# Attention with 128 weight columns for the scores, loads moved in the loop, and a rearranged passage from attention to the first expert block

## The chip, the cores and the metric

The kernel runs on one core of a Trainium2 chip. The metric is device microseconds of one execution; the kernel before has a median of 965.54 us in 3 runs (964.71 to 966.51). TensorE is written PE in the profile (PEld is its weight loads), VectorE DVE, ScalarE ACT, GpSimd POOL, SyncE SP.

## The reference

Causal attention over 4 batches, 12 heads, 448 positions and 64 dimensions a head, then two mixture-of-experts layers in sequence, each with 1792 tokens of 768 numbers, 8 experts, one expert a token, and 1024 hidden numbers. Everything is float32.

```
scores = where(causal, scale * q @ k.T, -1e9)
x      = softmax(scores) @ v                      # 1792 x 768
idx, gate = argmax / softmax of x_normed @ emb_normed.T / tau
x      = gate * (relu(x @ w1[idx]) @ w2[idx])     # first layer
idx, gate = argmax / softmax of x @ w_gate + bias[modality]
out    = gate * (relu(x @ w1'[idx]) @ w2'[idx])   # second layer
```

The routing of the first layer needs whole tokens, that is all twelve heads of a batch.

## The kernel before, in words

Attention works on 24 pairs of heads (`NPR`; six pairs a batch), each in four chunks of 112 query rows (`CP`). float32 products are made of two float32r parts, hi and lo: `split_pair` (L365) scales q and splits k and q on GpSimd, `split_v` (L379) splits v into three bfloat16 parts there. One round g of the loop from L763 works on four pairs at once: scores of pair g (`qk`, row maxima on VectorE, exponentials on ScalarE), the probabilities of pair g-1 as two float16 halves (`halves_hi` on ScalarE, `halves_lo` L424 on VectorE with both inputs in SBUF, DMA transposes of them on SP, and `last_chunk`, which transposes the last chunk on TensorE), the products with v of pair g-2 (`values`, then `combine`, which divides by the sums and writes x), and routing of pair g-3 (`route_t`: x transposed and split into xTh and xTl; `route_l`: its product with the expert embedding). Rounds 24 to 26 have no scores and finish the last pairs.

In `qk`, a chunk's scores are three products of q's 112 columns as weights (hi*hi, hi*lo, lo*hi), for two heads on the two halves of the rows, and one product of a 112 x 112 identity with the mask. hi and lo come from the pool `raw` with three buffers each; `r`, where k and q land, has four (`ld_p`), and v six.

The order of work is written out by hand: each engine and each DMA queue runs its instructions in program order. The loads of pair g+4 and of v of pair g+3 stand near the end of round g (L834 to L837), on SP's queue behind the transposes of `halves_hi(g)`. A batch's routing (`route1`, L629) is a generator; `tick` (L648) takes one step of it after certain VectorE operations, six in the rounds behind the last scores. `yield ALIGN` holds it until the top of the next round, where its products are put on TensorE. Its first part (`route_root`) takes roots of the squared norms, its second the expert of each token, ranks among the tokens of an expert, the softmax, counts, and four scatters by GpSimd. Batch b's routing starts when x of all its chunks has been stored and squared (`store_x`, `route_ss`, L808 to L816); for the third batch (b = 2) chunks 0, 1 and 2, 3 go out at the first, second and third round of the next batch.

From round 18 on, w1 of the expert with most tokens so far is loaded in six parts (`w1r`). Its float32r high parts `w1h` and low parts `w1l` are tiles of the pool `wb`, which is opened in round 24 when the memory of attention's probabilities is given back. GpSimd copies `w1h` 0 and 1, ScalarE 2 to 5; VectorE subtracts `w1l` 0 and 1 at the end of round 24 and 2, 3 and 4, 5 at the top of rounds 25 and 26. `warm` (L747) puts products of a constant on TensorE whose result nobody reads: eight (`WT`) in each of rounds 24 to 26, and six more (`WV`) ahead of `values` in rounds 24 and 25. `up` (L924) is the first product of an expert block: per half, 18 products of 512 columns, in the order L930, L931, L932 for each of six parts; L932 needs the low part of x (`xl`, L915 in `prep`).

Of the kernel before, what the change touches and what calls it, by code (L numbers as in the profile page):

```python
# [9 lines left out]
F32 = mybir.dt.float32  # L10
F32R = mybir.dt.float32r
BF16 = mybir.dt.bfloat16
# [3 lines left out]
AF = mybir.ActivationFunctionType  # L16
ALU = mybir.AluOpType
AX = mybir.AxisListType
# [5 lines left out]
P = 128  # L24
B, H, S, HD = 4, 12, 448, 64
CP, NCH = 112, 4
NT, D, F, E = 1792, 768, 1024, 8
KD, KF = D // P, F // P
# [13 lines left out]
WT = 8  # L42
WV = 6
# [12 lines left out]
def attention_two_moe_kernel(  # L56
# [34 lines left out]
    pool.memset(mask, 0.0)  # L91
    pool.affine_select(out=mask[:, :CP], in_=mask[:, :CP], compare_op=ALU.is_ge, fill=NEG, base=0,
                       pattern=[[-1, CP]], channel_multiplier=1)
    identb = const.tile([CP, CP], BF16, name="identb")
    vec.tensor_copy(identb, ident[:CP, :CP])
    iota_i = const.tile([P, JB * E], I32, name="iota_i")
    iota8 = const.tile([P, E], F32, name="iota8")
    pool.iota(iota_i[:, :E], pattern=[[1, E]], base=0, channel_multiplier=0)
# [43 lines left out]
    def pcopy(dst, src):  # L142
        pool.tensor_scalar(out=dst, in0=src, scalar1=1.0, scalar2=1.0, op0=ALU.mult, op1=ALU.mult)
# [149 lines left out]
    xb_p = right(st_v, "xb_p", 2)  # L293
    at_p = right(st_x, "at_p", 1)
    ld_p = right(st_q, "ld_p", 4)
    raw = right(st_q, "raw", 3)
    ps_s = st_q.enter_context(tc.tile_pool(name="ps_s", bufs=4, space=PSUM, side="right", reuse_waits="tile"))

    def clear_meta():
# [51 lines left out]
    PB = H // 2  # L351
    raws, spl, vrs, vss = {}, {}, {}, {}

    def load_pair(g):
        b, i = divmod(g, PB)
        r = ld_p.tile([P, 2, S], F32, tag="r", name=f"r{g}")
        nc.sync.dma_start(r, kqP[b, :, i])
        raws[g] = r

    def load_v(g):  # L360
        b, i = divmod(g, PB)
        vrs[g] = av_p.tile([CP, 2, NCH, HD], F32, tag="vr", name=f"vr{g}", bufs=6)
        nc.sync.dma_start(vrs[g], vh[b, :, 2 * i : 2 * i + 2])

    def split_pair(g, fast=False):  # L365
        r = raws.pop(g)
        (vec if fast else pool).tensor_scalar(out=r[:, 1], in0=r[:, 1], scalar1=-0.125, scalar2=1.0,
                                              op0=ALU.mult, op1=ALU.mult)
        hi = raw.tile([P, 2, S], F32R, tag="hi", name=f"hi{g}")
        lo = raw.tile([P, 2, S], F32R, tag="lo", name=f"lo{g}")  # L370
        spl[g] = hi[:, 0], lo[:, 0], hi[:, 1], lo[:, 1]
        if fast:
            vec.tensor_copy(hi, r)
            vec.tensor_sub(lo, r, hi.bitcast(F32))
        else:
            pcopy(hi, r)
            psub(lo, r, hi.bitcast(F32))
# [13 lines left out]
    def qk(g, c):  # L391

        kh, kl, qh, ql = spl[g]
        n = CP * (c + 1)
        cs = slice(c * CP, (c + 1) * CP)
        for e in range(2):
            scs[2 * g + e, c] = ps_s.tile([CP, 512], F32, tag="sc", name=f"sc{2 * g + e}_{c}")
        for st, (a, b) in enumerate(((qh, kh), (qh, kl), (ql, kh))):
            for e in range(2):
                rs = slice(e * HD, (e + 1) * HD)  # L400
                pe.matmul(scs[2 * g + e, c][:, :n], lhsT=a[rs, cs], rhs=b[rs, :n], start=(st == 0), stop=False)
        for e in range(2):
            pe.matmul(scs[2 * g + e, c][:, cs], lhsT=identb, rhs=mask[:, :CP], start=False, stop=True)  # L403

    def rowmax(h, c):
        if c == 0:
            nms[h] = sm_p.tile([CP, NCH], F32, tag="nm", name=f"nm{h}")
        vec.tensor_reduce(out=nms[h][:, c : c + 1], in_=scs[h, c][:, : CP * (c + 1)], axis=AX.X, op=ALU.min)  # L408

    def expo(h, c):  # L410
        n = CP * (c + 1)
        dst = exs[h // 2 % NEX][:, h % 2, boff[c] : boff[c] + c + 1].rearrange("p j k -> p (j k)")
        act.activation(dst, scs.pop((h, c))[:, :n], AF.Exp, bias=nms[h][:, c : c + 1], scale=-1.0)  # L413

    def transposed(dst, src):
        nc.sync.dma_start_transpose(dst[:, : 2 * ND * CP].rearrange("p (n q) -> p n q", q=CP),
# [264 lines left out]
    def split_w(which, his=None, los=None):  # L681
        drain(split_steps(which, his, los))
# [64 lines left out]
    def warm(ps, tag, n):  # L747

        wt = ps.tile([P, 512], F32, tag=tag, name="warm")
        for _ in range(n):  # L750
            pe.matmul(wt, lhsT=ones[:CP], rhs=mask, start=True, stop=True)
# [10 lines left out]

    for g in range(NPR + 3):  # L763
        t, v, r = g - 1, g - 2, g - 3
        if r == 0:
            drain(routing)
            routing = None
            vec.tensor_scalar_mul(tau_h, tau_t, 0.5)
            for b in range(B):
                vec.tensor_copy(mts[b][:, :, 3], mod_i[:, b * NCH : (b + 1) * NCH, 0])  # L770
# [7 lines left out]
        if g < NPR:  # L778
            for c in range(2):
                both(rowmax, g, c)  # L780
            for c in range(2):
                both(expo, g, c, ticks=False)
        if g == NPR + 1:
            split_w(1, (), (2, 3))
        if g == NPR + 2:
            split_w(1, (), (4, 5))
        if 0 <= t < NPR:
            halves_lo(t)
        next(late[0], None)
        if NPR <= g:  # L790
            warm(ps_T, "T", WT)
        if 0 <= r < NPR:
            if r == NPR - 1:
                for c in range(NCH):
                    route_ss(B - 1, c, xbs[B - 1], 2)
                last_root = route_root(B - 1)
                next(last_root)
            route_t(r, xbs[r // PB])
            if r == NPR - 2:
                for c in range(NCH):  # L800
                    route_ss(B - 1, c, xbs[B - 1], 1)
        next(late[0], None)
        if 0 <= v < NPR:
            if g > NPR - 1:
                warm(ps_T, "T", WV)
            values(v, 0)
        next(late[0], None)
        if PB <= r < NPR and r % PB < NCH:  # L808
            b = r // PB - 1
            c = -1  # L810
            for c in ((0,), (1,), (2,), (3,))[r % PB] if b < B - 2 else ((0,), (1,), (2, 3), ())[r % PB]:
                store_x(b, c)
                route_ss(b, c, xbs[b])
            if c == NCH - 1:
                drain(routing or ())
                routing = route1(b)  # L816
# [14 lines left out]
            combine(v, xbs[v // PB])  # L831
        if g < NPR:
            halves_hi(g)
        if g + 4 < NPR:  # L834
            load_pair(g + 4)
        if g + 3 < NPR:
            load_v(g + 3)  # L837
        if g + 2 < NPR:
            split_pair(g + 2)
        if g + 1 < NPR:  # L840
# [4 lines left out]
        if g == NPR - 1:  # L845
            st_q.close()
            ps_h = left("ps_h", 2, space=PSUM)
            ps_T = left("ps_T", 2, space=PSUM)
        if g == NPR:
            st_x.close()  # L850
            wb = left("wb", 1)
            w1h = [wb.tile([P, F], F32R, name=f"w1h{c}") for c in range(KD)]
            w1l = [wb.tile([P, F], F32R, name=f"w1l{c}") for c in range(KD)]
            w2r = [wb.tile([P, D], F32, name=f"w2r{f}") for f in range(KF)]
            m1.gather_early((0,), 2 * S)
            load_lead(m1, 2)
        if g == NPR:
            for k in range(2):
                pcopy(w1h[k], w1r[k])
            split_w(1, (2, 3, 4, 5), (0, 1))  # L860
    drain(routing)
    b = B - 1
    for c in range(NCH):
# [575 lines left out]
```

## Time and profile before

| | |
|---|---|
| median of 3 runs | 965.54 us (964.71 to 966.51) |
| profiled execution | 968.53 us, span 966.8 us |
| mean granted TensorE clock | 0.967 |
| busy: PE, PEld, DVE | 881.5, 761.0, 698.4 us |
| busy: ACT, POOL | 430.2, 472.4 us |
| scores of pair 0 start, of pair 23 end | 7.90, 242.8 us |
| first `up` starts | 275.23 us |

The profiled execution's span is from its first to its last instruction; the rest of its time lies around it. In a timeline a row gives the start in us from the span's start, the time it lasts, the engine, the line, the operation with output and inputs, and how many instructions were merged (x4); in brackets the idle time of the engine just before it and what ended it. In a busy table by stretch, the columns are the length, the busy time and count of PE, PEld, DVE, ACT and POOL, the granted clock, the DMA engines' share and GB/s.

### The profile page before, as it was taken

What the parts mean: (1) busy time and instruction counts of PE and PEld (TensorE: products, weight loads), DVE (VectorE), ACT (ScalarE), POOL (GpSimd) and SP (SyncE); (2) the same over time, 40 slices, a digit from 0 to 9 for tenths busy, and PEclk for the clock granted to TensorE, in tenths of its full rate; (3) what the DMA queues carried; (4) which work ended last, traced back from release to release, by engine and by line L of the source; (5) the groups of instructions that cost most, each with busy time, mean ns of one, the idle gap of its engine ahead of it and who ended that gap; (6) DMA issues with size and microseconds to landing.
All of it is one profiled execution on the core that took longest, in us unless ns stands there. A gap on an engine that the chain in (4) does not pass through costs nothing. (4 is left out here: it accounts for less than half of the span.)

```text
span 966.8 us, 20984 instructions
## 1 busy us (share of the span) xinstructions
PE 881.5 (91%) x7034; PEld 761.0 (79%) x7034; DVE 698.4 (72%) x1791; ACT 430.2 (44%) x777; POOL 472.4 (49%) x477
## 2 busy tenths in 40 slices
PE   5888988988879889999999999998989999899995
PEld 3777767767657778898988889886869988789894
DVE  6898988887784668589756865448757679996670
ACT  3656767756532465476524643245111234431211
POOL 8766574873145534365543563422534353453441
PEclk9899999988979999999999999999989999999998
DMA  6676977966815875468615563111172124411110
GB/s 181 139 161 128 193 153 157 198 158 167 244 61 188 290 273 187 166 210 301 234 57 165 187 213 104 52 37 38 53 251 98 37 65 166 152 46 43 59 44 32
DMA packets 112919, 137.47 MB, mean 142 GB/s; under 512 B 76820, under 2 KB 81226, under 8 KB 112752
## 3 DMA queue, kind: packets, MB, share of 16 engines
q1 hardware_dynamic: 99840, 108.75, 39.5%
q0 software_dynamic: 12912, 26.83, 8.6%
q8 instruction: 63, 1.03, 0.4%
q14 instruction: 104, 0.85, 0.3%
HBM read 101.48 MB, written 19.92 MB: 126 GB/s over the span
## 5 line engine op out<-in xcount | busy, mean ns | idle before, releaser
L728 POOL DMA_INDIRECT xg<-x,xi x128 | 135.1, 1055 | 105.2 <-DMA x<-yb,mg 55.1
L930 PE MATMUL h<-w1h,xh 128*128 128x512 f32 x408 | 165.8, 406 | 2.3 <-issue 0.8
L931 PE MATMUL h<-w1l,xh 128*128 128x512 f32 x408 | 163.4, 400 | 4.7 <-DVEq L1247 2.7
L932 PE MATMUL h<-w1h,xl 128*128 128x512 f32 x408 | 162.6, 399 | 0.5 <-issue 0.5
L992 PE MATMUL o<-w2l,hh 128*128 128x384 f32 x528 | 136.8, 340 | 4.6 <-DVE w2l L678 2.4
L992 PE MATMUL o<-w2h,hh 128*128 128x384 f32 x528 | 139.4, 345 | 1.8 <-issue 1.6
L992 PE MATMUL o<-w2h,hl 128*128 128x384 f32 x528 | 137.3, 341 | 3.3 <-issue 2.8
L972 DVE STREAM_TRANSPOSE hs<-h 32x256 f32<-32x256 f32 x240 | 107.0, 446 | 26.4 <-PE h L932 15.4
L413 ACT ACTIVATE ex<-sc,nm 112x112 f32<-112x112 f32 (+1 forms) x192 | 83.8, 492 | 77.2 <-DVE nm L408 75.8
L992 PEld LDWEIGHTS o<-w2l,hh 128*128 128x128 f32 x528 | 95.8, 189 | 7.1 <-issue 3.7
L992 PEld LDWEIGHTS o<-w2h,hl 128*128 128x128 f32 x528 | 96.4, 190 | 3.6 <-issue 2.5
L992 PEld LDWEIGHTS o<-w2h,hh 128*128 128x128 f32 x528 | 95.1, 190 | 4.8 <-issue 2.9
L978 ACT ACTIVATE hh<-hs 128x512 fp32r<-128x512 f32 x30 | 18.6, 631 | 177.0 <-PE o L992 122.5
L931 PEld LDWEIGHTS h<-w1l,xh 128*128 128x128 f32 x408 | 78.0, 191 | 23.7 <-DVE w1l L678 5.1
L930 PEld LDWEIGHTS h<-w1h,xh 128*128 128x128 f32 x408 | 78.2, 192 | 18.6 <-issue 2.6
L932 PEld LDWEIGHTS h<-w1h,xl 128*128 128x128 f32 x408 | 77.9, 191 | 18.8 <-issue 1.2
L678 DVE TENSOR_TENSOR w1l<-w1r,w1h 128x1024 fp32r<-128x1024 f32 x66 | 76.5, 1220 | 13.7 <-ACT w1h L676 11.8
L408 DVE TENSOR_REDUCE nm<-sc 112x1 f32<-112x112 f32 (+1 forms) x192 | 75.5, 440 | 12.1 <-PE sc L403 9.9
L678 DVE TENSOR_TENSOR w2l<-w2r,w2h 128x768 fp32r<-128x768 f32 x82 | 72.5, 953 | 4.9 <-ACT w2h L676 4.1
L903 DVE STREAM_TRANSPOSE xr<-xg 128x768 f32<-128x768 f32 x32 | 52.0, 1625 | 30.2 <-DMA xg<-x,xi 11.7
L676 ACT CAST w1h<-w1r 128x1024 fp32r<-128x1024 f32 x64 | 62.3, 1046 | 12.8 <-DMA w1r<-in_w1a 6.2
L1002 POOL DMA_INDIRECT out<-yb,mg x13 | 14.9, 1149 | 98.3 <-ACT yb L997 98.3
(306 smaller groups left out, 1981.5 us busy)
## 6 DMA issues: line engine op xcount, KB each, us to landing
w1r<-in_w1a SPq DMA_DIRECT2D x48, 512.0 KB
w2r<-in_w2a SPq DMA_DIRECT2D x64, 384.0 KB
r<-in_kqP SPq DMA_DIRECT2D x24, 448.0 KB
w1r<-in_w1b SPq DMA_DIRECT2D x18, 512.0 KB
w2r<-in_w2b SPq DMA_DIRECT2D x24, 384.0 KB
vr<-in_vh SPq DMA_DIRECT2D x24, 224.0 KB
x<-xb SPq DMA_DIRECT2D x16, 336.0 KB
xg<-x,xi POOLq DMA_INDIRECT x128
```

The lines of the kernel that those rows point to most:

```text
L408: vec.tensor_reduce(out=nms[h][:, c : c + 1], in_=scs[h, c][:, : CP * (c + 1)], axis=AX.X, op=ALU.min)
L413: act.activation(dst, scs.pop((h, c))[:, :n], AF.Exp, bias=nms[h][:, c : c + 1], scale=-1.0)
L676: act.copy(hi[k], r[k])
L678: vec.tensor_sub(lo[k], r[k], hi[k].bitcast(F32))
L728: pool.indirect_dma_start(out=xgs[j % 3][:, q * (D // Q) : (q + 1) * (D // Q)], out_offset=None, in_=quarters, in_offset=IND(ap=xi[:, q : ...
L903: vec.transpose(xr.rearrange("p k (q r) -> p q k r", q=Q), xgs[j % 3].rearrange("p (q r k) -> p q k r", q=Q, k=KD))
L930: pe.matmul(hps, lhsT=xh[:, c], rhs=w1h[c][:, ns], start=(c == 0), stop=False)
L931: pe.matmul(hps, lhsT=xh[:, c], rhs=w1l[c][:, ns], start=False, stop=False)
L932: pe.matmul(hps, lhsT=xl[:, c], rhs=w1h[c][:, ns], start=False, stop=(c == KD - 1))
L972: vec.transpose(hr[cols, :, rows], hps[rows, q * 256 : (q + 1) * 256].rearrange("p (c k) -> p k c", c=QR))
L978: act.activation(hh[k], part, AF.Relu)
L992: pe.matmul(ops[:, n, :384], lhsT=h[f // KH][:, f % KH], rhs=w[f][:, n * 384 : (n + 1) * 384], start=(f == 0 and st == 0), stop=(f == KF - ...
```

## The change

1. `hi` and `lo` become three fixed tiles each with 16 more columns, which are filled with zeros at the start; scores take 128 weight columns of q instead of 112 (the 16 columns behind the chunk belong to the next one or to the padding), the identity becomes 112 x 128, and the score tiles have 128 rows, of which 112 are read.
2. `load_pair(g + 4)` and `load_v(g + 3)` move from the end of round g to its top.
3. The third batch stores and squares chunks 0, 1 and 2, 3 at the first and second round, and its routing starts there, one round sooner.
4. `w1h` gets a pool of its own, opened in round 23; GpSimd's two copies are issued at its end. ScalarE's copies 2, 3 are issued at the end of round 24 and 4, 5 in round 25; VectorE's `w1l` 0 to 2 in round 25 and 3 to 5 at the end of round 26.
5. Of the 36 warming products 12 are left: six in round 25 behind `route_t`, six in round 26 ahead of it.

```
+    identb = const.tile([CP, P], BF16, name="identb")
-    raw = right(st_q, "raw", 3)
+    raw = right(st_q, "raw", 1)
+    his, los = ([raw.tile([P, 2 * S + P - CP], F32R, name=f"{nm}{i}") for i in range(3)] for nm in ("hi", "lo"))
+    for t in his + los:
+        for k in range(0, P - CP, E):
+            vec.tensor_copy(t[:, 2 * S + k : 2 * S + k + E], zero8)
...
-        spl[g] = hi[:, 0], lo[:, 0], hi[:, 1], lo[:, 1]
+        hi, lo = his[g % 3], los[g % 3]
+        spl[g] = hi[:, :S], lo[:, :S], hi[:, S:], lo[:, S:]
...
-                pe.matmul(scs[2 * g + e, c][:, :n], lhsT=a[rs, cs], rhs=b[rs, :n], start=(st == 0), stop=False)
+                pe.matmul(scs[2 * g + e, c][:, :n], lhsT=a[rs, c * CP : c * CP + P], rhs=b[rs, :n], start=(st == 0), stop=False)
...
     for g in range(NPR + 3):
         t, v, r = g - 1, g - 2, g - 3
+        if g + 4 < NPR:
+            load_pair(g + 4)
+        if g + 3 < NPR:
+            load_v(g + 3)
...
-        if g == NPR + 1:
-            split_w(1, (), (2, 3))
-        if g == NPR + 2:
-            split_w(1, (), (4, 5))
...
-        if NPR <= g:
-            warm(ps_T, "T", WT)
+        if g == NPR + 2:
+            warm(ps_T, "T", WV)
...
+        if g == NPR + 1:
+            split_w(1, (4, 5), range(3))
+            warm(ps_T, "T", WV)
...
-            if g > NPR - 1:
-                warm(ps_T, "T", WV)
             values(v, 0)
...
-            for c in (...)[r % PB] if b < B - 2 else ((0,), (1,), (2, 3), ())[r % PB]:
+            for c in (...)[r % PB] if b < B - 2 else ((0, 1), (2, 3), (), ())[r % PB]:
...
-        if g + 4 < NPR:
-            load_pair(g + 4)
-        if g + 3 < NPR:
-            load_v(g + 3)
...
             ps_T = left("ps_T", 2, space=PSUM)
+            wh, w1l = left("wh", 1), ()
+            w1h = [wh.tile([P, F], F32R, name=f"w1h{c}") for c in range(KD)]
+            for k in range(2):
+                pcopy(w1h[k], w1r[k])
         if g == NPR:
+            split_w(1, (2, 3), ())
             st_x.close()
             wb = left("wb", 1)
-            w1h = [wb.tile([P, F], F32R, name=f"w1h{c}") for c in range(KD)]
...
-        if g == NPR:
-            for k in range(2):
-                pcopy(w1h[k], w1r[k])
-            split_w(1, (2, 3, 4, 5), (0, 1))
+        if g == NPR + 2:
+            split_w(1, (), range(3, KD))
```

## Rows read from the trace of the kernel before

**Rows 1.** Busy time of each engine by stretch (us, busy, count), two stretches of attention

```profile
46.17:121.72 75.55, 66.91 (x1185) 54.81 (x1185) 65.91 (x144) 50.82 (x112) 47.75 (x39) 1.00 0.76 155
172.65:189.89 17.24, 16.41 (x297) 13.55 (x296) 14.62 (x37) 13.68 (x31) 13.24 (x14) 1.00 1.02 187
```

**Rows 2.** Timeline of DVE and POOL at two pairs (start, us, engine, line, operation)

```profile
77.57 3.24 DVE L426 SCALAR_TENSOR_TENSOR al<-ex,ah 112x672 f16<-112x672 f32 x2
78.56 1.53 POOL L146 TENSOR_TENSOR r<-r 112x512 bf16<-112x512 f32 x1
...
174.09 1.04 POOL L146 TENSOR_TENSOR r<-r 112x512 bf16<-112x512 f32 x1
175.27 1.62 DVE L426 SCALAR_TENSOR_TENSOR al<-ex,ah 112x672 f16<-112x672 f32 x2
```

**Rows 3.** Timeline of PE, POOL and DVE around pair 9's last scores

```profile
99.97 0.31 PE L403 MATMUL sc<-mask,identb 112*112 112x112 bf16 x2
...
101.70 0.56 POOL L367 TENSOR_SCALAR r<-r 128x448 f32<-128x448 f32 x1 [3.24 <-DMA r<-in_kqP]
102.34 0.94 POOL L143 TENSOR_SCALAR hi<-r 128x896 fp32r<-128x896 f32 x1
...
105.93 2.85 DVE L426 SCALAR_TENSOR_TENSOR al<-ex,ah 112x672 f16<-112x672 f32 x2
106.52 1.54 POOL L146 TENSOR_TENSOR r<-r 112x512 bf16<-112x512 f32 x1
```

**Rows 4.** Weight loads grouped by line and form (busy us, mean ns, idle before)

```profile
L930 PEld LDWEIGHTS h<-w1h,xh 128*128 128x128 f32 x408 | 78.2, 192 | 18.6 <-issue 2.6 <-ACT w1h L676 0.8
...
L401 PEld LDWEIGHTS sc<-hi 64*112 64x112 f32 x192 | 19.1, 179 | 27.0 <-DVE hi L373 7.9 <-issue 7.2 <-ACT ex L413 5.0
...
L403 PEld LDWEIGHTS <-identb 112*112 112x112 bf16 x192 | 17.8, 133 | 18.7 <-issue 14.6
...
L751 PEld LDWEIGHTS <-ones 112*128 112x128 bf16 x36 | 3.7, 106 | 3.9 <-issue 1.4
```

**Rows 5.** Timeline of DVE and ACT at pair 0

```profile
10.19 0.46 DVE L408 TENSOR_REDUCE nm<-sc 112x1 f32<-112x112 f32 x2 [0.98 <-PE sc L403]
11.09 0.84 ACT L330 ACTIVATE ebj<-eb 8x768 f32<-8x768 f32 x1 [9.02 <-DMA eb<-in_emb]
```

**Rows 6.** Timeline of DVE from attention's last pair to the first expert block

```profile
246.77 2.71 DVE L157 TENSOR_SCALAR rt_rr<-rt_sr 112x4 f32<-112x4 f32 x1
...
257.42 2.35 DVE L678 TENSOR_TENSOR w1l<-w1r,w1h 128x1024 fp32r<-128x1024 f32 x2
...
267.13 0.21 DVE L487 TENSOR_TENSOR xb<-t,rinv 112x64 f32<-112x64 f32 x1
...
268.01 2.35 DVE L678 TENSOR_TENSOR w1l<-w1r,w1h 128x1024 fp32r<-128x1024 f32 x2
...
271.32 0.62 DVE L507 TENSOR_TENSOR xTl<-t,xTh 128x448 fp32r<-128x448 f32 x1
...
276.27 1.02 DVE L915 TENSOR_TENSOR xl<-xt,xh 128x384 fp32r<-128x384 f32 x2 [0.57 <-ACT xh L914]
```

**Rows 7.** Timeline of POOL, PE and ACT in the same stretch

```profile
247.37 2.08 POOL L143 TENSOR_SCALAR w1h<-w1r 128x1024 fp32r<-128x1024 f32 x2
247.40 3.39 PE L751 MATMUL warm<-mask,ones 112*128 112x512 bf16 x8
...
255.09 3.87 ACT L676 CAST w1h<-w1r 128x1024 fp32r<-128x1024 f32 x4
...
260.69 0.74 ACT L540 ACTIVATE r1jk<-xb 112x640 f32<-112x640 f32 x1
...
268.81 0.53 ACT L506 CAST xTh<-t 128x448 fp32r<-128x448 f32 x1 [5.13 <-PE t L503]
...
276.88 0.80 PE L932 MATMUL h<-w1h,xl 128*128 128x512 f32 x1 [0.47 <-issue]
```

**Rows 8.** Busy time by stretch, `up` of the first block

```profile
275.00:280.00 5.00, 4.51 (x10) 2.66 (x9) 4.26 (x29) 2.03 (x4) 3.48 (x8) 0.50 0.05 6
```

More of the change, by code (lines that the diff above doesn't have):

```diff
@@ L93, in attention_two_moe_kernel @@
                        pattern=[[-1, CP]], channel_multiplier=1)
-    identb = const.tile([CP, CP], BF16, name="identb")
-    vec.tensor_copy(identb, ident[:CP, :CP])
+    identb = const.tile([CP, P], BF16, name="identb")
+    vec.tensor_copy(identb, ident[:CP])
     iota_i = const.tile([P, JB * E], I32, name="iota_i")
@@ L368, in split_pair @@
                                               op0=ALU.mult, op1=ALU.mult)
-        hi = raw.tile([P, 2, S], F32R, tag="hi", name=f"hi{g}")
-        lo = raw.tile([P, 2, S], F32R, tag="lo", name=f"lo{g}")
-        spl[g] = hi[:, 0], lo[:, 0], hi[:, 1], lo[:, 1]
+        hi, lo = his[g % 3], los[g % 3]
+        spl[g] = hi[:, :S], lo[:, :S], hi[:, S:], lo[:, S:]
+        r = r.rearrange("p k s -> p (k s)")
+        hi, lo = hi[:, : 2 * S], lo[:, : 2 * S]
         if fast:
@@ L396, in qk @@
         for e in range(2):
-            scs[2 * g + e, c] = ps_s.tile([CP, 512], F32, tag="sc", name=f"sc{2 * g + e}_{c}")
+            scs[2 * g + e, c] = ps_s.tile([P, 512], F32, tag="sc", name=f"sc{2 * g + e}_{c}")
         for st, (a, b) in enumerate(((qh, kh), (qh, kl), (ql, kh))):
@@ L407, in rowmax @@
             nms[h] = sm_p.tile([CP, NCH], F32, tag="nm", name=f"nm{h}")
-        vec.tensor_reduce(out=nms[h][:, c : c + 1], in_=scs[h, c][:, : CP * (c + 1)], axis=AX.X, op=ALU.min)
+        vec.tensor_reduce(out=nms[h][:, c : c + 1], in_=scs[h, c][:CP, : CP * (c + 1)], axis=AX.X, op=ALU.min)
     def expo(h, c):
@@ L412, in expo @@
         dst = exs[h // 2 % NEX][:, h % 2, boff[c] : boff[c] + c + 1].rearrange("p j k -> p (j k)")
-        act.activation(dst, scs.pop((h, c))[:, :n], AF.Exp, bias=nms[h][:, c : c + 1], scale=-1.0)
+        act.activation(dst, scs.pop((h, c))[:CP, :n], AF.Exp, bias=nms[h][:, c : c + 1], scale=-1.0)
     def transposed(dst, src):
@@ L810, in attention_two_moe_kernel @@
             c = -1
-            for c in ((0,), (1,), (2,), (3,))[r % PB] if b < B - 2 else ((0,), (1,), (2, 3), ())[r % PB]:
+            for c in ((0,), (1,), (2,), (3,))[r % PB] if b < B - 2 else ((0, 1), (2, 3), (), ())[r % PB]:
                 store_x(b, c)
```

## The prediction

> **What bounds the kernel now.** I read the page's forty slices first: TensorE is at 9 tenths in nearly every slice behind the twelfth, which are the two mixture-of-experts stages. The diff touches nothing behind the first expert block, so only attention (0 to about 275 us) and the first products behind it are in question. Then I took two stretches of attention from the table of busy time by stretch [rows 1]. The eight pairs of heads from 46.17 to 121.72 take 75.55 us, 9.44 each, with VectorE busy 65.91; the two from 172.65 take 17.24, 8.62 each, with VectorE busy 14.62. Length less VectorE's time is 1.2 and 1.3 us a pair in both: one wait of VectorE on ScalarE. So **VectorE's own work plus one fixed wait sets a pair's length**, and TensorE fits beside it (16.41 of 17.24). At 8.62 the eight pairs would take 69.0; they lose 6.6 us.
>
> The timeline of VectorE and GpSimd says where [rows 2]. The two operations of `halves_lo` take 1.62 us together from 175.27, when GpSimd's split of v has just ended (174.09 + 1.04); at 77.57 they take 3.24, and the same split beside them takes 1.53.
>
> Behind attention I followed VectorE and TensorE to the first product that waits for everything, `up`'s first L932 at 276.88 [rows 7]. It needs the split x (276.27), which stands behind VectorE's last xTl (271.32), and that behind two w1 splits (268.01, 2.35 us) and the last x (267.13 + 0.21) [rows 6]. TensorE mostly waits there.
>
> **The change part by part.**
>
> *Loads at the top of the loop.* In SP's order `load_pair(g+4)` moves from behind pair g's transposes to ahead of the next iteration's, but there g is one more: the same slot fetches one pair further. Today GpSimd idles 3.24 us until its data lands at 101.70 [rows 3]. With the data a pair earlier it is held only by the buffers of hi and lo, which come free with pair 9's last score product, 99.97 + 0.31 = 100.3. Its split can start there; today (scale first) it starts at 102.34: 2.0 later. The train from there to the end of v's split, 106.52 + 1.54, is 5.72, of which 0.5 is stretching (1.04 is the undisturbed value [rows 2]). So it would end at 105.5, and `halves_lo`, which takes 2.85 now, starts at 105.93. The overlap goes. But the next pair's scale (0.56) then follows at once, its data being there, and in a shorter pair the gap of 0.4 shrinks. Between all 6.6 us and nothing I take somewhat under half: **-3.0**. Ends: -6.6, and +6.4 if all eight pairs had the 1.62 us extra of 77.57 (0.82 on average now). No queue is blocked by the move: the load's buffer was last read three pairs before, v's one pair before; only in the first rounds does the load wait for GpSimd's split, with nothing but later transposes behind it.
>
> A rule bears on this. The Trainium skill (SBUF — State Buffer, "Who interferes with whom") says that a VectorE instruction with two SBUF inputs and a GpSimd instruction that reads SBUF exclude each other for the whole instruction, and that one with a single SBUF input doesn't contend. The stretched `halves_lo` (both inputs in SBUF) agrees; by it the whole 6.6 would go wherever the train ends in time, and what still overlaps would be paid in full.
>
> *128 weight columns.* A load of 112 float32r columns for the scores takes 179 ns in the mean, 128 such columns in the expert blocks 192; the mask's 112 bf16 columns take 133, 128 bf16 columns in the warming products 106 [rows 4]. A pair has 12 score loads on each of two row halves side by side, 12 x 13 ns = +0.16 us, and 8 mask loads, 8 x 27 = -0.22. On the path over 24 pairs that would be -1.4 us (+3.8 with the first term alone, -5.2 with the second); beside VectorE it is **0**, which I take. If the cover goes, TensorE has 0.4 us a pair left in the short pairs.
>
> *Padding.* Six tiles get 16 columns by twelve small VectorE copies ahead of the first split. At an estimated 0.07 to 0.2 us each that delays VectorE by 0.8 to 2.4. The first row maxima (10.19, two in 0.46) would end at 11.5 or later instead of 10.65; ScalarE's exponentials wait for the embedding's square anyway, 11.09 + 0.84 [rows 5]. Most is hidden; that pair's later maxima slip: **+0.3** (0 to +1.5).
>
> *Third batch's routing one pair sooner.* Counting the generator's steps (8 ticks behind its start, then 16 a pair), the six root steps that begin at 246.77 now run inside pair 23. Four fall into waits there, two don't: +0.4. The transposes and ten small steps (0.2 us each) move to iteration 24, the ranks to the top of 25, softmax and counts into the last `combine`. Two chunks' stores and squares move a pair up, on SP ahead of the transposes of the next, on ScalarE into its wait for row maxima.
>
> *Own pool for w1's high halves, no warming products.* Today the root step at 246.77 takes 2.71 us, with GpSimd's two w1 copies (247.37, 2.08) beside it [rows 6, 7]; the copies now run right behind pair 23's last scores, some 3 us earlier. That frees 2.5 us of VectorE; the ten steps cost 2.0. From TensorE go 14 warming products in iteration 24 (eight alone 3.39 us). `combine(22)`, which ends just ahead of 257.5 today, I put 1.5 earlier: 256.0. From there ScalarE is last: rank products 0.3, transposes 0.5, xTh 0.53, four squares of 0.74, two w1 copies of 0.97 (3.87 for four), the routing's exponential 0.25 [rows 7]: 262.5. VectorE (w1 splits 0 to 2, 3.5 us) and TensorE (six warming products and pair 23's values) are done by 261.5. Then eight routing steps of 0.2, a reciprocal and the multiplications, 0.9, give the last x at 265.2, against 267.34: -2.1. The two w1 splits ahead of the last xTl are gone from there; behind transposes and xTh it starts at about 266.5 instead of 271.32: -4.8. Behind it now stand three w1 splits (3.5) and six root steps (1.3), then half of x's split (0.5): L932 at 272.5, against 276.88: -4.4, with the +0.4 above **-4.0** (-5 to +2.4, rival 2). Late next is VectorE, on which that product hangs. What follows (table, gathers, the second expert's weights) is released from there and moves along; the DMA engines are nearly idle then (0.05 [rows 8]).
>
> Sum: -3.0 + 0 + 0.3 - 4.0 = **-6.7 us**. The profiled execution took 968.53 (span 966.80, 1.73 around it), 3.0 above the median of 965.54; the sum gives 961.8 on its scale and **958.8** on the median's.
>
> **The rivals.**
> 1. *Only the end gets shorter.* GpSimd's train still meets `halves_lo`, as the scale joins its tail. For: the gap is 0.4 us, the scale 0.56. Against: today the overlap is nearly two whole operations. 965.5 + 0.3 - 4.0 = 961.8.
> 2. *The clock takes the end back.* Today TensorE runs at a granted 0.50, the 1.2 GHz level, from 275 to 280 [rows 8], after a stretch of few, spread products, in spite of the warming ones; some 15 of `up`'s 36 products are slow. A 512-column product takes 0.42 us slow (3.39 for eight [rows 7]) and half at the other level. If all 36 are slow: 21 x 0.21 = +4.4, and about +2 (an estimate by the same ratio) for pair 22's and 23's values. -4.0 + 6.4 = +2.4; with attention's -2.7 it is 965.2. For: two thirds of the warming products go. Against: the gaps between real products shrink too. The Trainium skill (TensorE: Matmul & The Clock Gate, "Why this matters for your kernels") advises against gaps between bursts of products; by it this is what taking their filling away does.
> 3. *Slower: GpSimd's train lands on `halves_lo`.* Place: every pair from 4 to 20. If the hi and lo buffers come free half a us or more later than I read (the train starts after 100.8), v's splits and the scale fall on `halves_lo` every time, and each pair has the 1.62 extra: +6.4 on the eight, and about +5 on the nine behind (two have none today). With the end's -3.7: 965.5 + 7.7 = 973.
> 4. *It doesn't do what it says.* The loads land no earlier because transposes fill the DMA queues (a share of 0.76, and 1.02 from 172.65 [rows 1]), and the first block waits for something that didn't move, such as GpSimd's scatters ahead of its gathers: 965.5 within 1.5.
>
> **How the numbers follow.** Forecast 0.45 (own range 954 to 962), rival 1 0.20, rival 2 0.13, rival 3 0.11, rival 4 0.11. A measurement of this kernel can tell about 0.2%, 1.9 us, from no change. Faster: forecast, rival 1, half of rival 2 and a part of rival 4, 0.76. Within: 0.13. Slower: rival 3, 0.11. The range: below, all of attention's 6.6, 5 at the end and a part of the masks' gain, 953; above, rivals 2 and 4, 966; rival 3 stays outside.
>
> **What would show it.** GpSimd's scale (L367) without waits for its data from pair 6 on; `halves_lo` at 1.7 to 2.3 us a pair between 46 and 122 and pairs of 8.7 to 9.2; score loads 13 ns longer, mask loads 27 shorter; root steps before 246 and none of 2.7 us; the last xTl 4 to 5 us earlier and L932 with it; the clock at 0.50 for no more of `up` than now. It is wrong if `halves_lo` stays above 2.5 us, if the embedding no longer covers the copies, or if the last `combine` waits for ScalarE past 264.

## The result and the profile after

The changed kernel takes **956.89 us** (median of 4 runs, 955.57 to 959.19) against 966.02 beside it: ratio 0.9909, interval 0.9887 to 0.9931. A second comparison gave 950.26 against 958.27, ratio 0.9912 (0.9882 to 0.9942). That is 9.1 and 8.0 us less; the forecast was 6.7 less. Each comparison below has its own runs of the kernel before, on the same chip, so only ratios are compared; one per mille is about 1 us. Single runs of the kernel before lay between 952.9 and 964.9 in one of them, so a ratio is known to about 0.3%, and the stages of the traces say more than the times.

The profiled execution took 957.3 us, with a span of 955.6 against 966.8. Its busy time by stretch has the same eight pairs as the first stretch of [rows 1], pairs 12 to 22, the way from pair 23's first score to `up`'s first product with the low part of x (L932 before, L937 now; the expectations call it the first of `up`'s third pass, the text below the way behind attention), and from there to the first `down` product, which is the second product of the expert block (columns: stretch, its length, then busy time and count of PE, PEld, DVE, ACT and POOL, granted clock, DMA share, GB/s):

```profile
49.48:119.67 70.19, 65.32 (x1186) 53.55 (x1185) 59.99 (x145) 51.46 (x113) 44.45 (x37) 1.00 0.91 167
119.67:230.92 111.25, 99.03 (x1647) 80.35 (x1647) 94.70 (x263) 75.41 (x163) 76.74 (x71) 0.94 0.76 170
230.92:268.60 37.68, 27.83 (x412) 21.78 (x411) 29.12 (x94) 20.94 (x41) 10.56 (x15) 0.86 0.74 208
268.60:280.55 11.95, 11.03 (x47) 8.22 (x47) 10.93 (x56) 4.89 (x9) 4.23 (x7) 0.87 0.02 3
```

Before, the same four are 75.55, 112.07, 43.09 and 12.67. Pairs 4 to 11 lose 5.4 us and the way behind attention 5.4 more; the first pairs take 3.3 of it back (pair 4 starts at 49.48 instead of 46.17). The profile of the kernel before is an extreme one in two of these numbers: in the other thirteen profiles below pair 4 starts at 48.2 to 51.2, and the way behind attention takes 40.4 to 40.5 in the four others that have the old end. Length less VectorE's time is 1.28 us a pair in pairs 4 to 11, 1.21 before: VectorE still sets a pair's length, it only has less to do. The sixteen `halves_lo` operations of those pairs, in one row for after and one for before (columns: stretch, length, VectorE's time in that line, clock, DMA share, GB/s):

```profile
49.48:119.67 70.19, 15.30 (x16) 1.00 0.91 167
```

```profile
46.17:121.72 75.55, 21.51 (x16) 1.00 0.76 155
```

6.2 us less, 1.91 a pair instead of 2.69. GpSimd's and VectorE's timelines of one pair after show why:

```profile
91.09 0.94 POOL L143 TENSOR_SCALAR hi<-r 128x896 fp32r<-128x896 f32 x1 [2.34 <-PE sc L409]
92.11 2.15 POOL L146 TENSOR_TENSOR lo<-r,hi 128x896 fp32r<-128x896 f32 x1
94.21 1.05 POOL L146 TENSOR_TENSOR r<-vr 112x512 f32<-112x512 f32 x1
95.34 1.04 POOL L146 TENSOR_TENSOR r<-r 112x512 bf16<-112x512 f32 x1
96.35 1.17 POOL L372 TENSOR_SCALAR r<-r 128x448 f32<-128x448 f32 x1
90.45 1.97 DVE L414 TENSOR_REDUCE nm<-sc 112x1 f32<-112x336 f32 x4
96.21 2.01 DVE L432 SCALAR_TENSOR_TENSOR al<-ex,ah 112x672 f16<-112x672 f32 x2
```

In [rows 3] the train waited 3.24 us for its data and ended beside `halves_lo`. Now it waits for the pair's last score product, which frees the hi buffer, and v's split has ended 0.2 us after `halves_lo` begins. What is left of the overlap is the scale: it takes 1.17 us instead of 0.56, and `halves_lo` 2.01 instead of 1.62 [rows 2]. The rest of the train lies beside other work of VectorE. Its four row maxima, which read the scores in PSUM, take no longer for it: 1.97 us at 90.45, and 1.97 at 100.16 before, where GpSimd waited for its data until 101.70.

Behind attention, VectorE's row of 2.71 us in [rows 6] is gone, and the chain runs so (timeline of VectorE and TensorE):

```profile
254.55 3.49 DVE L684 TENSOR_TENSOR w1l<-w1r,w1h 128x1024 fp32r<-128x1024 f32 x3
258.90 0.18 DVE L182 TENSOR_REDUCE fr_smr<-fr_shr 112x4 f32<-112x32 f32 x1 [0.69 <-ACT fr_shr L178]
260.71 0.20 DVE L493 TENSOR_TENSOR xb<-t,rinv 112x64 f32<-112x64 f32 x1
262.23 0.62 DVE L513 TENSOR_TENSOR xTl<-t,xTh 128x448 fp32r<-128x448 f32 x1 [0.16 <-issue]
262.77 3.49 DVE L684 TENSOR_TENSOR w1l<-w1r,w1h 128x1024 fp32r<-128x1024 f32 x3
267.99 1.02 DVE L920 TENSOR_TENSOR xl<-xt,xh 128x384 fp32r<-128x384 f32 x2 [0.56 <-ACT w2h L692]
268.60 0.79 PE L937 MATMUL h<-w1h,xl 128*128 128x512 f32 x1 [1.43 <-DVE xl L920]
```

The last x is there at 260.91 (267.34 before), the last xTl starts at 262.23 (271.32), L937 at 268.60 (276.88). VectorE waits from 254.55 on 0.69 us for ScalarE's exponential, 0.16 ahead of the last xTl and 0.56 ahead of the split x; the last of these is 0.56 or 0.57 us with the old end and the new. TensorE waits 1.43 us for the split x, which stands on VectorE behind three w1 splits (3.49 us): these are what `up` hangs on.

### The profile page after: what moved, and what is told of

Read it like the earlier page. It is cut to its first block, busy times and chain, and to the rows that moved or that the text cites. A ratio compares the mean times of both kernels' runs of the same rounds, so it can differ in the third digit from the quotient of the medians.

```text
span 955.6 us, 20950 instructions
## 1 busy us (share of the span) xinstructions
PE 874.7 (92%) x7010; PEld 760.8 (80%) x7010; DVE 694.1 (73%) x1803; ACT 430.9 (45%) x777; POOL 475.6 (50%) x477
## 5 line engine op out<-in xcount | busy, mean ns | idle before, releaser
L937 PE MATMUL h<-w1h,xl 128*128 128x512 f32 x408 | 161.7, 396 | 1.4 <-DVE xl L920 1.4
L937 PEld LDWEIGHTS h<-w1h,xl 128*128 128x128 f32 x408 | 77.4, 190 | 20.1 <-DVE xl L920 2.4
L935 PEld LDWEIGHTS h<-w1h,xh 128*128 128x128 f32 x408 | 77.5, 190 | 18.2 <-issue 1.9
L414 DVE TENSOR_REDUCE nm<-sc 112x1 f32<-112x112 f32 (+1 forms) x192 | 75.6, 437 | 10.1 <-PE sc L409 9.5
```

The source lines that it names most:

```text
L414: vec.tensor_reduce(out=nms[h][:, c : c + 1], in_=scs[h, c][:CP, : CP * (c + 1)], axis=AX.X, op=ALU.min)
L935: pe.matmul(hps, lhsT=xh[:, c], rhs=w1h[c][:, ns], start=(c == 0), stop=False)
L937: pe.matmul(hps, lhsT=xl[:, c], rhs=w1h[c][:, ns], start=False, stop=(c == KD - 1))
```

## Experiments

One profile of each kernel isn't enough to read a stage: pair 2 lasts 11.4 to 14.3 us in the fourteen profiles, whatever the kernel. So the stages are compared over all of them. The runs e1 to e4 are one comparison, after_again and e5 to e7 a second, e8 to e11 a third, each on another chip; the changed kernel itself ran in the second of them only. "With the loads" means at the top of the loop.

### The loads alone (e1_loads)

```diff
         t, v, r = g - 1, g - 2, g - 3
+        if g + 4 < NPR:
+            load_pair(g + 4)
+        if g + 3 < NPR:
+            load_v(g + 3)
...
-        if g + 4 < NPR:
-            load_pair(g + 4)
-        if g + 3 < NPR:
-            load_v(g + 3)
```

> The kernel before with the loads moved to the top of the loop and nothing else. Theory (the loads give attention's whole gain: GpSimd's split is then held by the hi and lo buffers and not by its data): pairs 4 to 11 take about 70.2 us instead of 75.55, halves_lo falls to about 1.7 us a pair there, the start and the end stay, and the time is 966.0 - 5.4 = 960.6 us. Rival (the 128 weight columns, with mask loads 34 ns shorter, shorten the pairs): pairs 4 to 11 stay above 74.5 us and the time is within 1 us of 966.

Measured: 950.65 against 955.05, ratio 0.996 (0.9931 to 0.999); the theory's 960.6 of 966.0 is 0.9944. Its pairs 4 to 11 and 12 to 22 (the way behind attention takes 40.53):

```profile
48.77:119.12 70.35, 65.85 (x1185) 54.30 (x1184) 60.11 (x145) 51.49 (x113) 44.33 (x37) 1.00 0.88 167
119.12:233.45 114.33, 101.04 (x1648) 83.03 (x1648) 96.79 (x263) 75.25 (x162) 75.12 (x70) 0.93 0.76 161
```

The eight pairs fall to 70.35 without any column edit: the loads give the whole of that stage, and the rival fell. `halves_lo` takes 1.92 us a pair there (1.7 expected). But pairs 12 to 22 take 114.3 us, and the gain of the time is smaller than the stage's.

### The pair's load alone (e11_pair_only)

As above, but `load_v` stays at its old place.

> The kernel before with load_pair alone at the top of the loop and load_v at its old place. Theory (GpSimd's train was late for the data of keys and queries): pairs 4 to 11 take 70.3 us, halves_lo 2.0 us a pair there, as with both. Rival (v's load counts as well, its split is the part of the train beside halves_lo): pairs 4 to 11 take 72 to 74 us.

Measured: pairs 4 to 11 take 70.22 us, `halves_lo` 1.91 us a pair there (15.24 for sixteen), pairs 12 to 22 112.92; the time 956.97 against 960.06, ratio 0.9983 (0.9957 to 1.0009). The data of keys and queries were what GpSimd's train was late for, and v's load may stay where it was, as far as the stage shows it; the time can't be told from no change.

### The changed kernel without the loads (e10_no_loads)

The changed kernel with the four lines back at the end of the loop.

> The changed kernel with the loads back at the end of the loop. Theory (the loads' 5.2 us come off in full, 0.0054): pairs 4 to 11 take 75.4 us, and the time is 0.9965 of the kernel before. Rival (pairs 12 to 22 take a part of the loads' gain back, since routing holds them up at a fixed place): pairs 12 to 22 are 2 us or more shorter than the 111 with the loads, and the time is 0.994 or less.

```profile
49.13:124.28 75.15, 66.80 (x1186) 53.97 (x1185) 65.50 (x144) 50.80 (x112) 47.97 (x39) 1.00 0.78 155
124.28:234.01 109.73, 96.41 (x1647) 78.12 (x1647) 94.18 (x263) 76.73 (x166) 74.53 (x71) 0.97 0.85 178
143.10:156.10 13.00, 10.85 (x155) 8.76 (x154) 10.38 (x31) 8.16 (x17) 9.01 (x9) 0.87 0.61 108
```

959.84 against 960.06, ratio 0.9986 (0.9956 to 1.0016); the way behind attention takes 37.51 us. The theory's stage holds (75.15), and its 0.9965 lies in the interval. The rival's 0.994 doesn't, but its idea does: pairs 12 to 22 are shorter without the loads, by 1.5 us against the changed kernel's profile (2 expected) and by 2.2 in the means over all profiles. The third row is pair 14, 13.0 us at a granted 0.87. In the changed kernel the same pair, and two stretches of it (one before the clock falls, one behind):

```profile
138.07:153.57 15.50, 13.59 (x153) 10.97 (x152) 11.36 (x33) 8.54 (x17) 10.71 (x10) 0.67 0.44 91
140.00:142.00 2.00, 0.59 (x7) 0.32 (x5) 1.72 (x7) 1.49 (x3) 1.92 (x2) 1.00 0.00 0
144.00:146.00 2.00, 2.00 (x36) 1.97 (x35) 2.00 (x4) 1.11 (x3) 1.71 (x2) 0.50 0.96 210
```

This is a pair in which the routing of a finished batch runs. TensorE idles for 1.4 of 2 us, waiting for VectorE's `combine`, and then the values of the pair run at 1.2 GHz. Over the fourteen profiles pairs 14 and 15 together take 23.9 to 26.3 us with the loads (nine profiles, mean 24.7) and 22.4 to 23.0 without (five, mean 22.7): **2.0 us of the loads' gain come back there.** In seven of the nine the two pairs have a mean granted clock of 0.79, against 0.85 to 0.92 without the loads. In the two longest, e1 and e4 (25.81 and 26.32 us), it is 0.87, but VectorE is busy for 20.8 and 21.7 us instead of 18.2 to 18.8: a cast of the routing that takes 0.3 to 0.6 us in the other profiles falls beside GpSimd's split (e4_pad_act; the same cast takes 1.71 in e1_loads):

```profile
148.59 2.14 POOL L146 TENSOR_TENSOR lo<-r,hi 128x896 fp32r<-128x896 f32 x1
149.01 1.76 DVE L595 CAST r1ohbr<-am_ohr 112x32 bf16<-112x32 f32 x1
```

So a longer half-clock stretch goes with the loss in seven profiles, and a stretched VectorE in two. Pairs 4 to 11 take 70.2 to 70.6 with (mean 70.3) and 74.9 to 75.6 without (75.2).

### The columns alone (e2_cols), and the change without them (e5_no_cols)

The first is the kernel before with the diff's edits to `identb`, to the hi and lo tiles (padding included) and to the score tiles and their readers; the second is the changed kernel with these undone:

```diff
-    identb = const.tile([CP, P], BF16, name="identb")
-    vec.tensor_copy(identb, ident[:CP])
+    identb = const.tile([CP, CP], BF16, name="identb")
+    vec.tensor_copy(identb, ident[:CP, :CP])
...
-                pe.matmul(scs[2 * g + e, c][:, :n], lhsT=a[rs, c * CP : c * CP + P], rhs=b[rs, :n], start=(st == 0), stop=False)
+                pe.matmul(scs[2 * g + e, c][:, :n], lhsT=a[rs, cs], rhs=b[rs, :n], start=(st == 0), stop=False)
```

> The kernel before with 128 weight columns and the padding copies, and nothing else. Theory (TensorE's loads lie beside VectorE, the copies push VectorE's first split into GpSimd's): the first score product comes 1.9 us later, pair 2 starts about 3.5 us later, pairs 4 to 11 stay at 75.6 +- 0.7 us, score loads take 18 ns more and mask loads 34 less, and the time is 966.0 + 3.3 = 969.3 us. Rival (the shorter mask loads carry attention's gain): pairs 4 to 11 take 70 to 71 us and the time is 963.5.

> The changed kernel with 112 weight columns again and no padding: the loads and the end alone. Theory (the columns are worth nothing on the path, the copies cost VectorE 1.3 us ahead of its first split): pairs 4 to 11 stay at 70.2 us, the time is 1.3 us below the changed kernel's, 0.989 to 0.992 of the kernel before. Rival (mask loads that are 34 ns shorter are on TensorE's path now that pairs take 8.77 us): pairs 4 to 11 take 71 us or more and the time is 1 us or more above the changed kernel's.

The columns alone: 956.87 against 955.05, ratio 1.0027 (0.9996 to 1.0058), not told from no change nor from the theory's 3.3 us more; pairs 4 to 11 take 75.42, as the theory had it, pair 2 starts at 27.12. The change without them: 949.56 against 958.27, ratio 0.9907 (0.9878 to 0.9935), the changed kernel beside it 0.9912. Its way behind attention takes 35.75 us, its pairs 4 to 11:

```profile
50.60:121.10 70.50, 65.82 (x1186) 54.29 (x1185) 60.20 (x145) 51.44 (x113) 44.22 (x37) 1.00 0.91 165
```

128 columns gain nothing that these runs can tell. The weight loads themselves moved as foreseen: their groups after in pairs 4 to 11 (busy us, mean ns; before in the same pairs 173 and 128 ns):

```profile
L407 PEld LDWEIGHTS sc<-lo,hi 64*128 64x128 f32 x66 | 6.3, 186 | 0.0
L409 PEld LDWEIGHTS <-identb 112*128 112x128 bf16 x64 | 3.6, 97 | 5.5 <-issue 4.1
```

### The padding on ScalarE (e4_pad_act)

```diff
     for t in his + los:
         for k in range(0, P - CP, E):
-            vec.tensor_copy(t[:, 2 * S + k : 2 * S + k + E], zero8)
+            act.copy(t[:, 2 * S + k : 2 * S + k + E], zero8)
```

> The kernel after with the twelve padding copies on ScalarE, which waits there for the embedding, instead of VectorE. Theory (the start's +3.3 us are the copies' 1.3 and 2.1 of VectorE's first split stretched because it slipped under GpSimd's): VectorE's first split starts at about 6.8, the low half ends at about 9.3 instead of 12.6, pair 2 starts near 24.6 instead of 28.15, and the time is 956.9 - 3.3 = 953.6 us. Rival (pair 2 waits for GpSimd's split of v either way, or the head start is given back in the next pairs): pair 4 starts within 1 us of 49.5 and the time is 956 to 957.

First the changed kernel's start (VectorE, GpSimd), then this one's (VectorE, GpSimd, ScalarE, TensorE):

```profile
7.23 0.93 DVE L357 CAST lo<-zero 128x8 fp32r<-128x8 f32 x6
8.48 1.24 DVE L379 CAST hi<-r 128x896 fp32r<-128x896 f32 x1
9.76 2.84 DVE L380 TENSOR_TENSOR lo<-r,hi 128x896 fp32r<-128x896 f32 x1
9.33 2.32 POOL L146 TENSOR_TENSOR lo<-r,hi 128x896 fp32r<-128x896 f32 x1
```

```profile
7.24 0.63 DVE L379 CAST hi<-r 128x896 fp32r<-128x896 f32 x1
7.90 1.33 DVE L380 TENSOR_TENSOR lo<-r,hi 128x896 fp32r<-128x896 f32 x1
8.38 1.65 POOL L143 TENSOR_SCALAR hi<-r 128x896 fp32r<-128x896 f32 x1
11.99 0.84 ACT L330 ACTIVATE ebj<-eb 8x768 f32<-8x768 f32 x1 [4.58 <-DMA eb<-in_emb]
26.67 0.84 PE L407 MATMUL sc<-hi 64*128 64x112 f32 x2 [2.24 <-ACT ex L419]
```

949.54 against 955.05, ratio 0.9948 (0.9918 to 0.9978), above both the theory's 0.987 and the rival's 0.990; the changed kernel's 0.9909 and 0.9912 are from other comparisons, and the intervals overlap. VectorE's split is 3.4 us sooner, as the theory had it, but then the embedding lands late (11.99 instead of 11.09 in [rows 5]) and ScalarE's first exponentials stand behind its square: pair 2 starts at 26.67, not 24.6, and pair 4 at 48.70, within the rival's 1 us. The kernel e3_end below has no copies at all, and its first split is stretched just as much, since the data of GpSimd's split of pair 1 landed earlier (its scale starts at 6.60, at 7.27 in the kernel before, whose first instructions are the same and whose subtraction takes 1.33):

```profile
6.60 0.57 POOL L367 TENSOR_SCALAR r<-r 128x448 f32<-128x448 f32 x1 [1.10 <-DMA r<-in_kqP]
8.28 2.32 POOL L146 TENSOR_TENSOR lo<-r,hi 128x896 fp32r<-128x896 f32 x1
8.71 2.84 DVE L374 TENSOR_TENSOR lo<-r,hi 128x896 fp32r<-128x896 f32 x1
```

Where GpSimd's long subtraction is issued first (9.33 ahead of 9.76, 8.28 ahead of 8.71), VectorE's takes 2.84 us; where VectorE's comes first (7.90), it takes 1.33, and GpSimd's copy beside it 1.65 instead of 0.94. The Trainium skill (SBUF — State Buffer, "Who interferes with whom") says that the order of issue decides who is blocked, for the whole instruction; these rows agree.

### The end alone (e3_end) and w1's pool alone (e9_pool_only)

The first is all of the diff's end; the second of it only:

```diff
         if g == NPR - 1:
...
+            wh, w1l = left("wh", 1), ()
+            w1h = [wh.tile([P, F], F32R, name=f"w1h{c}") for c in range(KD)]
+            for k in range(2):
+                pcopy(w1h[k], w1r[k])
...
-            w1h = [wb.tile([P, F], F32R, name=f"w1h{c}") for c in range(KD)]
...
-            for k in range(2):
-                pcopy(w1h[k], w1r[k])
```

> The kernel before with the new end alone (own pool for w1's high halves, fewer warming products, the third batch's routing one pair sooner). Theory (VectorE's chain to the split x shortens): the first product of the third pass of up comes 5.4 us sooner behind the start of pair 23 (43.1 to 37.7), the half clock ends sooner too, and the time is 966.0 - 5.4 - 0.7 = 959.9 us. Rival (the clock takes part of it back without the warming products): TensorE is at half clock for longer than 5 us behind that product, and the time is 963 or more.

> The kernel before with w1's high halves in their own pool and GpSimd's two w1 copies behind pair 23's last scores; the splits and the warming products stay at their old places. Theory (GpSimd's copies no longer stand beside VectorE and ScalarE in iteration 24, which cost about 2.6 us there): up's third pass starts near 38 us behind pair 23's first score instead of 40.5 or 43.1, and the time is 0.9965 to 0.998 of the kernel before. Rival (the rearranged splits of w1 are the gain of the end): 40 us or more, and 0.999 to 1.001.

The end alone: 952.56 against 955.05, ratio 0.9985 (0.996 to 1.0011). The way behind attention takes 37.25 us, as the theory had it, with 3.8 us at half clock behind that product (the rival wanted more than 5); but the theory's time, 0.9937, lies outside the interval, and no gain of the time can be told. The pool alone: 958.74 against 960.06, ratio 0.9971 (0.9936 to 1.0005); the way takes 40.37, as with the old end (40.43 to 43.09 in four profiles). The theory fell by the stage; the time tells it neither from its rival nor from no change. Timeline of e9_pool_only, then of e8_loads_pool below, which has no warming products there (both have the third batch's routing at its old place):

```profile
245.04 0.16 DVE L157 TENSOR_SCALAR rt_rr<-rt_sr 112x4 f32<-112x4 f32 x1
246.02 3.20 PE L751 MATMUL warm<-mask,ones 112*128 112x512 bf16 x8
249.06 0.55 PE L503 MATMUL t<-ident,xb 112*128 112x112 f32 x4
250.21 0.62 DVE L507 TENSOR_TENSOR xTl<-t,xTh 128x448 fp32r<-128x448 f32 x1 [2.56 <-ACT xTh L506]
```

```profile
243.18 0.16 DVE L157 TENSOR_SCALAR rt_rr<-rt_sr 112x4 f32<-112x4 f32 x1
245.72 0.62 DVE L507 TENSOR_TENSOR xTl<-t,xTh 128x448 fp32r<-128x448 f32 x1
```

The root step takes 0.16 us instead of 2.71, and VectorE then waits 2.56 for xTh: the transposes stand in TensorE's queue behind eight warming products. The two lay beside one another in the kernel before, and taking one away shows the other: from the start of the root step to that of xTl it is 5.17 us in e9 and 5.19 in the kernel before. Without the warming products of that round it is 2.54 (e8, and e7 below), so 2.6 us of the end's gain come from there. Whether the rearranged w1 splits have a share in the rest no run tells apart.

Nor was it the pool that shortened the root step. In e1, e2 and e11, with the old end, it takes 0.16 us as well. With the old end it is stretched only in the profile of the kernel before, where pair 23 ran partly at the lower clock (granted 0.87) and the step came 2.6 us later, beside GpSimd's copies. The stretch from pair 23's first score to the root step, in the kernel before and in e1_loads:

```profile
233.79:246.77 12.98, 9.85 (x149) 8.26 (x148) 9.02 (x26) 10.14 (x22) 2.47 (x3) 0.87 0.67 157
233.45:243.85 10.40, 8.29 (x149) 6.79 (x148) 8.94 (x24) 9.01 (x20) 2.33 (x3) 1.00 0.87 179
```

That is also most of the way of 43.09 instead of 40.4 to 40.5.

### Without the last warming products (e6_no_warm), with the routing late (e7_route_late), and the changed kernel again (after_again)

```diff
-        if g == NPR + 2:
-            warm(ps_T, "T", WV)
...
             split_w(1, (4, 5), range(3))
-            warm(ps_T, "T", WV)
```

```diff
-            for c in ((0,), (1,), (2,), (3,))[r % PB] if b < B - 2 else ((0, 1), (2, 3), (), ())[r % PB]:
+            for c in ((0,), (1,), (2,), (3,))[r % PB] if b < B - 2 else ((0,), (1,), (2, 3), ())[r % PB]:
```

> The changed kernel once more, beside the next three, because the kernel before took 955 us in the last comparison and 966 in the first. Theory (the gain is made in two places that no chip's speed touches, 5.2 us in pairs 4 to 11 and 3 to 5 behind pair 23): pairs 4 to 11 take 70.2 us, up's third pass starts 37.5 us behind pair 23's first score, and the time is 0.990 to 0.993 of the kernel before. Rival (the first comparison was lucky; with the start 2 to 3 us later only loads and end together less that remain): 0.995 to 0.997.

> The changed kernel without the twelve warming products that it still has. Theory (the clock falls here with or without them, and the real products bring it back): the half clock ends within 1 us of where it does in the changed kernel, up's third pass starts within 0.5 us of 37.5 behind pair 23's first score, and the time is within 1 us of the changed kernel's. Rival (the warming products hold the clock): TensorE stays at half clock for 3 us or more longer through up's first products, and the time is 2 to 4 us above the changed kernel's.

> The changed kernel with the third batch's routing at its old iteration, one pair later. Theory (moving it sooner takes ten small steps and the transposes from VectorE's last chain): up's third pass starts 1.5 to 2.5 us later behind pair 23's first score (39 to 40), and the time is 2 us above the changed kernel's. Rival (the steps fall into waits either way, as the prediction's +0.4 for moving them sooner had it): up's third pass within 0.5 us of 37.5, the time 0.4 below the changed kernel's.

Ratios: again 0.9912; without warming 0.9911 (0.9879 to 0.9942); routing late 0.991 (0.9878 to 0.9942). The changed kernel's stages are there again, as its theory had them: 70.15 us in pairs 4 to 11 and 37.53 behind attention. Without warming the latter is 37.93, within the theory's half us. Three stretches of 5 us, of after_again and then of e6_no_warm:

```profile
255.00:260.00 5.00, 5.00 (x111) 3.74 (x109) 4.27 (x11) 4.35 (x11) 0.00 (x0) 1.00 0.97 360
260.00:265.00 5.00, 1.97 (x10) 0.90 (x10) 4.67 (x19) 1.05 (x2) 4.15 (x7) 0.78 0.61 188
270.00:275.00 5.00, 5.00 (x21) 3.61 (x21) 4.74 (x27) 0.10 (x1) 0.00 (x0) 0.69 0.02 5
```

```profile
255.00:260.00 5.00, 2.49 (x70) 2.02 (x66) 4.27 (x11) 4.41 (x11) 0.00 (x0) 0.95 0.98 371
260.00:265.00 5.00, 2.09 (x6) 0.86 (x6) 4.26 (x20) 1.05 (x2) 4.10 (x7) 0.50 0.57 174
270.00:275.00 5.00, 5.00 (x21) 3.61 (x21) 4.90 (x29) 0.00 (x0) 0.00 (x0) 0.68 0.00 2
```

Without the twelve products the clock falls some 3 us sooner, in a stretch where TensorE waits anyway, and comes back at the same place. They are worth nothing that can be measured. Nor is the routing's move: with it late, the way behind attention takes 35.44 us (expected 39 to 40), and pairs 20 to 22 take 33.8. From the start of pair 20 to L937 that is 69.3 us together, where the six other profiles with both the loads and the new end have 69.0 to 71.1. Both of my numbers for it missed.

### The loads and the pool with its splits alone (e8_loads_pool)

The kernel before with e1_loads's edit and the end's, but no warming products behind attention, the old routing place and 112 columns.

> The kernel before with two edits alone: the loads at the top of the loop, and the own pool for w1's high halves with its splits; no warming products behind attention, the third batch's routing at its old place, 112 weight columns without padding. Theory (these two carry the whole gain, the other three edits nothing that can be measured): pairs 4 to 11 take 70.4 us, up's third pass starts 35 to 38 us behind pair 23's first score, and the time is 0.989 to 0.992 of the kernel before. Rival (the edits that are worth nothing one at a time are worth something together): 0.994 or more.

Measured: 954.54 against 960.06, ratio 0.9933 (0.9904 to 0.9962); pairs 4 to 11 70.36 us, the way behind attention 37.21. Both stages are the changed kernel's, the ratio lies between the two theories' ranges and its interval holds 0.9912. So the rival, that the other edits add something together, isn't ruled out. No version was found that is measurably faster than the changed kernel; e5_no_cols and e8_loads_pool can't be told from it and have less.

## Why the prediction was right, step by step

The starts of the first `down` product of the first expert block show each part ahead of what no edit touches. They are 289.55, 286.29 and 287.52 with neither loads nor the new end (before, e2, e9: mean 287.8); 286.40 and 284.60 with the loads alone (e1, e11: 285.5); 285.16 and 283.60 with the end alone (e3, e10: 284.4); and 280.55 to 283.10 with both (seven profiles: 281.6). The loads give 2.3 to 2.8 there, the end 3.4 to 3.9, together **6.2**; the sum had 6.7. Within one group the starts lie up to 3.3 us apart, so that each part is known to 1 or 2 us only. That the total came so near owes something to luck, as the parts show:

- *Loads, -3.0.* The mechanism was right (`halves_lo` 1.91 us a pair, pairs of 8.6 to 9.0, GpSimd's scale without a wait), its size in the stage was 4.9, and the step lacked a term: 2.0 come back in pairs 14 and 15, at the lower clock or with routing's steps stretched. At pair 23's first score the loads are worth 1.9 (232.4 in the mean of nine profiles, 234.3 of five; pair 4 starts 0.8 later in the mean of the nine, which the early start of the kernel before makes). The forecast of somewhat under half was near the net and wrong on both parts. I had read only pairs that run at full clock for this step.
- *Columns, 0.* Right: score loads 13 ns longer, mask loads 31 shorter, pairs 4 to 11 unmoved.
- *Padding, +0.3.* The cover that the step relied on is gone: the first exponentials wait 1.10 us for the row maxima behind the embedding's square, as the prediction's own sign of being wrong had it. Pair 2 starts at 28.1 in the five profiles that have the copies on VectorE and their first split stretched, at 24.6 to 28.0 in the others. The copies take 1.3 us; the rest depends on when the data of pair 1 and of the embedding land, which differs by 1 us and more between runs. At pair 4 little of it is left: 49.8 in the mean of the six profiles with copies on VectorE, 49.3 of the eight others. In the times it can't be seen (e4, e5).
- *Routing sooner.* Worth nothing, within what a ratio can tell.
- *End, -4.0.* The way behind attention is 41.0 us in the mean of five profiles with the old end (40.4 without the kernel before's) and 37.1 of nine with the new: 3.9 (3.4). But the 2.5 us freed on VectorE, which the step counted first, were a row of that one profile and lay beside the wait for the transposes, so they were worth nothing as long as eight warming products stood before these (e9). The sum took the warming products away as well, so its total held, with the wrong part counted first.
- *Rivals.* Rival 1 fell with the 70.19 us, rival 2 with the profile after and e6: the clock is back at full at 271.9 instead of 281.8, 5 us behind L932 before and 3 behind L937 after. Rival 3 didn't come about: the hi buffer comes free when I read it to. Its price was too high in any case: it took 0.82 us a pair as what `halves_lo` had too much already, but by its own line that was 1.07 (2.69 less 1.62), which leaves 4.4 on the eight pairs instead of 6.4. Rival 4 fell with both stages. Rival 2's idea, that the lower clock takes a gain back, came up in another place, pair 14. The Trainium skill (TensorE: Matmul & The Clock Gate, "Why this matters for your kernels") advises against gaps between bursts, and means longer ones than here. In pair 14 of the changed kernel TensorE idled for 1.56 us in one piece, and yet the granted clock fell to 0.50 behind it; whether this gap made it fall no run shows. At the end filling gaps gained nothing (0.9911 without the twelve products, 0.9912 with them).
- *The rule on shared reads.* The prediction's sentence from the Trainium skill (SBUF — State Buffer, "Who interferes with whom") leaves out an exception that the section makes, for VectorE's 2-port modes. For a single SBUF input the sentence as it stands doesn't hold here: the root step of [rows 6] and the cast in e4 have one each and took 2.71 and 1.76 us beside GpSimd, 0.16 and 0.3 to 0.6 elsewhere. For `halves_lo`, with two, the rows bear it out.

Two things stay open. Why shorter pairs are mostly followed by a longer half-clock stretch in pairs 14 and 15 is not settled; in the kernel before and in the changed one it began behind a wait of TensorE for `combine`, 1.55 and 1.56 us long. And of the 8 to 9 us in the times, 6.2 stand ahead of the first `down` product. The ratios of single parts don't add up to 0.991 either: loads alone and end alone, 0.996 and 0.9985, make 0.9945, and e4, which has all edits (the copies on ScalarE) and ran beside them, 0.9948. Within the intervals of 0.3% both can be so. Behind the first `down` product the span still has 664 to 677 us in the fourteen profiles, for code that no edit touches, so a remainder of 2 us can't be placed.

## What to carry to other kernels

Read a stage's gain on to the next fixed point: here 4.9 us in eight pairs were 1.9 at the end of attention. Before counting a freed wait, look at what else ends at the same time: one of two waits side by side is worth nothing alone. Look for the row in a second profile too: the stretched root step stood in one of five. Where a kernel's time spreads by more than the effect, repeat the profile with other edits undone, and compare the stage over all of them.

## What the hardware showed that I had not expected

- Runs with the same first instructions differ in when the first tiles land (GpSimd's first scale starts at 6.60 us in e3, 7.27 in the kernel before, 8.20 in e9), and with that the same VectorE subtraction takes 2.84, 1.33 and 1.09 us.
- Stretching is mutual: GpSimd's scale takes 0.56 us alone and 1.17 beside `halves_lo`, its first operation on v 1.04 alone and 1.88 at the changed kernel's start, beside VectorE's subtraction. VectorE's row maxima, which read PSUM, took 1.97 us beside GpSimd and without it.
- A mean granted clock of 0.97 for the span says little: the same two pairs, 14 and 15, take 22.4 to 26.3 us with a granted clock of 0.79 to 0.92, and the longest are not those with the lowest.
